# Weight sums of one stream in two steps, eight warming products, and a new written order

## The chip, the cores and the metric

One Trainium2 chip, one core of it. The metric is the device time of one execution in microseconds; the median of the runs shown is compared. The core has TensorE for matrix products (PE, with PEld for loading its stationary operand), VectorE (DVE), ScalarE (ACT), GpSimd (POOL) and SyncE (SP), which issues most of the DMAs. Products are written to PSUM, everything else lives in SBUF.

## The reference

A causal convolution in time with 15 taps and a spacing of 2, from 144 to 288 channels, over 2 sequences of 16000 positions; then the gate tanh(f) * sigmoid(g) on the two halves of the 288 channels, and a product with a 144 x 144 matrix. Inputs and output are bfloat16.

```python
xp = jnp.pad(x, ((0, 0), (pad, 0), (0, 0)))          # pad = 28
h = sum(einsum('btc,cd->btd', xp[:, pad-2*i : pad-2*i+T], w[i]) for i in range(15))
z = tanh(h[..., :144]) * sigmoid(h[..., 144:])
out = z @ w_o
```

## The kernel before, in words

The positions are cut into 11 blocks, and these into 21 units. A unit takes 128 runs of 12 positions each (one run per partition) through the convolution, the gate and the projection. The convolution is not computed tap by tap: it is split like a fast polynomial product. Sums and differences of shifted inputs are formed on VectorE, sums and differences of weights once at the start, and TensorE needs fewer products for the same result. The four streams are S, D, F and G. S works on the sum of two shifted inputs with the sums of the weights of taps j and j + 8 (G1); D on the differences (Gm); F and G on the difference E with the plain weights. Each stream has derived inputs (S2, S4, S42 and so on, made by `derive`) and derived weights:

- G1 (Gm for D): w[j] plus (minus) w[j + 8], for j = 0 to 6; the eighth is w[7] alone.
- H: G1[j] - G1[j + 4], for j = 0 to 3.
- HH: G1[j] - G1[j + 4] - G1[j + 2] + G1[j + 6], for j = 0 and 1.
- GD: G1[4h + j] - G1[4h + j + 2], for h and j = 0 and 1.

The weights of D, F and G are made by VectorE (`wsum`, line 550, "ws" in the order). Those of S are made by TensorE: `psum_sum` (line 560) multiplies plain weights with the identity or its negative, so that the sum comes up in a PSUM pair, and a cast on ScalarE puts it into SBUF ("wsum" in the order, first the products, then the cast). In the kernel before, each of the nine sums takes plain weights alone, and each waits for all four loads of w (`load_w`, line 529; slice q holds taps 4q to 4q + 3, the last slice three taps).

In a unit the steps of a stream k are named VVk (two products with HH), V2ak and V2bk (with H), cVVk and cVk (ScalarE's negated copies inside PSUM), AVk (with GD), A00k to A11k (with G1 or w; a last "r" marks the product with the rest channels), and evk, yk (results out of PSUM). The 16 input channels above 128 are kept apart: their sums ("st") are transposed and laid out as R. For block 0 that happens on TensorE (`sums_front`, line 403): 16 transposes ("trR", line 420), a copy of one half by ScalarE and one by VectorE ("cpR", line 427), and two products with zeros ("zR", line 432) that reset the PSUM pair, for r = 0 and again for r = 1. For other blocks it goes through DMAs (T, q, R). Wr holds the weights of the rest channels, loaded by 15 DMAs on POOL ("wrl"), wo_ab those of the projection ("wol"). "OP" is the projection, "os" its cast, "th", "sg" and "zm" the gate.

PSUM is divided into four pairs of banks; a step that opens a pair waits until all users of the pair's former content are done. The order on every engine's queue is a written list (`ORDER`, lines 33 to 116), one list each for PE, ACT, DVE, DMA (SP's queue), POOL and for the opening of pairs. A name is unit/step; unit -1 is the preparation. `place` (line 200) takes the steps by these lists. The costs and due times given to `add` made the lists, and they do not change which step follows which.

Ahead of everything TensorE runs warming products of zeros, 512 columns each (line 527).

Of the kernel before, what the change touches and what calls it, by code (L numbers as in the profile page):

```python
# [26 lines left out]
def t_dve(n, psum=False):  # L27
# [7 lines left out]
   -1/wsum#10 wsum#6 wsum#12 wsum#4 wsum#16 wsum#8 wsum#2 wsum wsum#14 0/VVF V2bF V2aF VVG -1/trR 0/V2aG V2bG A01F A11F -1/zR 0/A10F A00F A00G A11Fr  # L35
   A01G A10Fr A00Fr A10G A01Fr A11G A00Gr A01Gr 1/AVS 0/VVS A11Gr A10Gr AVS V2aS V2bS -1/trR#1 0/A00S A01S A11S A00Sr A01Sr -1/zR#1 0/A10S VVD A10Sr
   A11Sr AVD V2aD V2bD 1/VVS 0/A01D A00D A01Dr A00Dr 1/V2aS V2bS 0/A11D A10D A11Dr A10Dr 1/A00S A01S A10S AVD VVD A11S V2aD V2bD VVF A10D A11D A00D
   A01D V2bF V2aF VVG 2/AVS 1/A00F A01F V2bG V2aG A10F A11F A11G 2/VVS 1/A10G A00G 2/V2bS V2aS 1/A01G 2/AVD A01S A00S VVD A10S A11S V2bD V2aD 1/OP0
   2/VVF A11D A10D A00D A01D V2aF V2bF 3/AVD 2/VVG A01F A00F A10F V2bG V2aG A11F 1/OP1 2/A00G 3/VVS 2/A01G A11G A10G 3/V2aS V2bS AVS VVD A11S A10S V2bD
   V2aD A01S A00S VVF A01D A00D A11D A10D V2bF V2aF 2/OP0 3/VVG A11F A10F 4/AVS 3/V2bG V2aG A01F A00F 2/OP1 3/A00G 4/VVS 3/A01G A10G A11G 4/V2bS V2aS  # L40
   AVD VVD A10S A11S V2aD V2bD A00S A01S VVF A01D A00D A11D A10D V2bF V2aF 5/AVD 4/VVG A11F A01F A00F A10F V2bG V2aG 3/OP1 OP0 4/A00G 5/VVS 4/A01G
   5/AVS V2bS V2aS 4/A10G A11G 5/VVD A11S A10S V2bD V2aD A00S A01S VVF A00D A01D A10D A11D V2bF V2aF 4/OP0 5/VVG A01F A00F 6/AVS 5/A10F A11F V2aG V2bG
   4/OP1 6/VVS 5/A11G A10G A00G A01G 6/V2aS V2bS AVD VVD A10S A11S V2bD V2aD A01S A00S VVF A11D A10D A01D A00D V2aF V2bF 7/AVD 6/VVG A01F A11F A00F
   A10F V2aG V2bG 5/OP1 OP0 6/A11G 7/VVS 6/A10G 7/AVS V2aS V2bS 6/A00G 7/VVD 6/A01G 7/A00S V2aD V2bD A01S A10S A11S A11D VVF A10D A01D A00D V2bF V2aF
   6/OP0 7/VVG A10F A11F 8/AVS 7/A01F A00F V2bG V2aG 6/OP1 8/VVS 7/A00G A01G 8/AVD V2aS V2bS 7/A10G 8/VVD 7/A11G 8/A01S A00S V2bD V2aD A10S A11S VVF
   A01D A00D A11D A10D V2bF V2aF 9/AVD 8/VVG A01F A11F A10F A00F V2bG V2aG 7/OP1 OP0 8/A11G A10G 9/VVS 8/A01G A00G 9/V2aS V2bS AVS VVD A11S A10S V2aD
   V2bD A00S A01S VVF A00D A01D A10D A11D V2bF V2aF 8/OP0 9/VVG A01F A11F A00F A10F 10/AVS 9/V2bG V2aG 8/OP1 10/VVS 9/A01G A00G 10/AVD V2aS V2bS 9/A10G
   10/VVD 9/A11G 10/A01S V2aD V2bD A00S A10S A11S A11D VVF A10D A01D A00D V2aF V2bF 11/AVD 10/VVG A10F A00F V2aG A11F 9/OP1 10/A01F V2bG 9/OP0 11/VVS
   10/A10G A11G A01G A00G 11/V2aS V2bS AVS VVD A11S A10S V2bD V2aD A00S A01S VVF A10D A11D V2bF V2aF A01D A00D 10/OP0 11/A10F VVG A01F 12/AVS 11/A11F
   A00F V2aG V2bG 10/OP1 12/VVS 11/A00G A01G 12/AVD V2bS V2aS 11/A11G 12/VVD 11/A10G 12/A01S V2bD V2aD A00S A10S A11S A00D VVF A01D A11D A10D V2aF V2bF  # L50
   13/AVD 12/VVG A10F A01F A11F A00F V2bG V2aG 11/OP1 OP0 12/A11G 13/VVS 12/A10G 13/AVS V2bS V2aS 12/A00G 13/VVD 12/A01G 13/A11S V2aD V2bD A10S A00S
   A01S A00D A01D VVF A11D A10D 12/OP0 13/V2bF V2aF VVG 14/AVS 13/A01F V2aG A00F V2bG A10F A11F 12/OP1 13/A00G 14/VVS 13/A01G 14/AVD V2bS V2aS 13/A11G
   14/VVD 13/A10G 14/A01S A00S V2bD V2aD A10S A11S VVF A10D A11D A01D A00D V2bF V2aF 15/AVD 14/VVG A01F V2bG A10F V2aG A11F A00F A10G 13/OP1 OP0
   14/A11G 15/VVS 14/A00G A01G 15/V2bS V2aS AVS VVD A00S A01S V2bD V2aD A11S A10S VVF A10D A11D A00D A01D V2bF V2aF 14/OP0 15/VVG A01F A00F 16/AVS
   15/V2aG A10F V2bG 14/OP1 15/A11F A10G 16/VVS 15/A11G 16/AVD V2bS V2aS 15/A01G A00G 16/VVD A11S A10S V2bD V2aD A01S A00S VVF A10D A11D A01D A00D V2aF
   V2bF 17/AVD 16/VVG A00F V2aG V2bG A01F A11F A10F A00G A01G 15/OP1 OP0 17/VVS 16/A10G A11G 17/V2aS V2bS AVS VVD A11S A10S V2aD V2bD A01S A00S VVF
   A01D A00D A11D A10D V2aF V2bF 16/OP0 17/VVG A00F A01F A10F 18/AVS 17/V2aG V2bG A11F 16/OP1 17/A00G 18/VVS 17/A01G 18/AVD V2bS V2aS 17/A11G A10G
   18/VVD A10S A11S V2aD V2bD A01S VVF A00S A01D A00D A11D A10D V2aF V2bF 19/AVD 18/VVG A01F A00F A11F A10F V2aG V2bG 17/OP1 OP0 18/A00G 19/VVS 18/A01G
# [186 lines left out]
def kernel(  # L245
# [7 lines left out]
    nc = tc.nc  # L253
    P = 128
# [267 lines left out]
    warm = const.tile([P, 1], F32)  # L522
    K_(nc.gpsimd.memset(warm[:], 0.0))
    K_(nc.scalar.activation(out=warm[:], in_=warm[:], func=ACT.Sigmoid))
    NWARM = 15
    for i in range(NWARM):
        K_(nc.tensor.matmul(banks[i % 4][:, (i // 4) % 2, :], lhsT=wz[:, 0:P], rhs=wz[:], start=True, stop=True))  # L527

# [468 lines left out]
```

## Time and profile before

| what | us |
|---|---|
| median of 3 runs (312.89 to 314.5) | 313.0 |
| profiled execution | 313.12 |
| its span | 311.3 |
| TensorE busy | 297.5 |
| VectorE busy | 276.5 |
| ScalarE busy | 269.0 |

The span runs from the first to the last instruction; the execution's time holds 1.8 us around it. Line numbers (L491, L316) are those of the kernel before. L491 is the helper that issues nearly all products, L316 the one for nearly all of VectorE's sums, so rows are told apart by their tiles: "acc<-w_all,ident" is a weight sum, "acc<-wz" at L527 a warming product, "acc<-ident,T" at L420 a transpose for R. In the timeline a row gives the start, the length and what the engine waited for.

### The profile page before, as it was taken

The numbers are of one execution on the slowest core, as the hardware profiler recorded it, in microseconds if no ns is written. First come the engines' busy times: TensorE is split into PE (matmuls) and PEld (weight loads), VectorE is DVE, ScalarE is ACT, GpSimd is POOL, SyncE is SP. The second block draws the span as 40 slices with busy tenths as digits, with TensorE's granted clock in tenths as the row PEclk, the third lists the DMA queues.
The fourth block names the chain that finished last, engine by engine and source line by source line (L and its number), as shares of the span: only waits on it lengthen the run. The fifth ranks groups of instructions, "written<-read, shape, count | busy, mean of one in ns | idle before, by whom it ended". The sixth has DMA issues, their size and how long they took to land.

```text
span 311.3 us, 6703 instructions
## 1 busy us (share of the span) xinstructions
PE 297.5 (96%) x2604; PEld 276.5 (89%) x2604; DVE 276.5 (89%) x393; ACT 269.0 (86%) x449; POOL 27.0 (9%) x63
## 2 busy tenths in 40 slices
PE   8998899999999999999999999999999999999981
PEld 3797789999999999999999999999999999999881
DVE  4878999999999999899999999989996998899861
ACT  1658789998989989999998999989888999989982
POOL 9830500000000000000000000000000000000013
PEclk9999999999999999999999999999999999999997
DMA  7995569597799866986796698455886647254344
GB/s 199 107 127 118 150 67 174 140 115 153 126 162 282 215 159 104 142 199 155 189 210 98 118 181 182 138 127 162 146 187 80 123 141 231 73 128 114 59 170 131
DMA packets 153110, 45.78 MB, mean 147 GB/s; under 512 B 137061, under 2 KB 151701, under 8 KB 153078
## 3 DMA queue, kind: packets, MB, share of 16 engines
q1 hardware_dynamic: 151610, 44.59, 69.6%
q0 software_dynamic: 1216, 0.70, 1.1%
q8 instruction: 20, 0.33, 0.5%
q14 instruction: 12, 0.10, 0.1%
q10 hardware_dynamic: 252, 0.06, 0.1%
HBM read 13.31 MB, written 11.84 MB: 81 GB/s over the span
## 4 chain that ended last, share of the span: by engine, by line
PE 80%; ACT 13%; DVE 3%; issue 3%; DVEq 0%; ACTq 0%
PE acc L491 77%; ACT m L761 4%; ACT acc L683 3%; PE acc L527 2%; ACT acc L677 1%; ACT sg L746 1%; ACT th L744 1%; ACT R L427 1%; DVE D L316 1%; DVE S L316 1%; PE acc L420 1%; DVE y L316 1%; ACT os L882 0%; ACT av L695 0%; ACT osl L852 0%
## 5 line engine op out<-in xcount | busy, mean ns | idle before, releaser
L491 PEld LDWEIGHTS <-E 128*128 128x128 bf16 x882 | 112.2, 145 | 7.9 <-issue 4.0
L491 PE MATMUL acc<-w_all,E 128*128 128x288 bf16 x630 | 101.2, 286 | 1.0 <-ACT acc L683 0.3
L491 PE MATMUL acc<-Wr,R 128*128 128x288 bf16 x336 | 94.9, 286 | 0.0
L316 DVE TENSOR_TENSOR y<-U,acc 128x576 bf16<-128x576 bf16 (+1 forms) x81 | 59.4, 744 | 9.9 <-PE acc L491 6.5
L683 ACT ACTIVATE acc<-acc 128x576 f32<-128x576 f32 x84 | 54.1, 645 | 7.2 <-PE acc L491 4.9
L761 ACT ACTIVATE m<-acc 128x576 bf16<-128x576 f32 x84 | 52.8, 651 | 4.3 <-PE acc L491 2.9
L491 PEld LDWEIGHTS <-S 128*128 128x128 bf16 x378 | 48.2, 137 | 5.2 <-issue 2.4
L491 PEld LDWEIGHTS <-D 128*128 128x128 bf16 x378 | 48.8, 137 | 4.0 <-issue 1.1
L677 ACT ACTIVATE acc<-acc 128x288 f32<-128x288 f32 x84 | 33.7, 401 | 8.0 <-PE acc L491 6.4
L746 ACT ACTIVATE sg<-y 128x576 bf16<-128x576 bf16 (+3 forms) x45 | 38.9, 872 | 0.5 <-DVE y L316 0.4
L744 ACT ACTIVATE th<-y 128x576 bf16<-128x576 bf16 (+3 forms) x45 | 38.9, 871 | 0.2
L882 ACT CAST os<-acc 128x864 bf16<-128x864 f32 x40 | 34.6, 880 | 2.0 <-DVE y L316 0.9
L316 DVE TENSOR_TENSOR m<-m,av 128x1152 bf16<-128x1152 bf16 x42 | 30.5, 753 | 6.5 <-ACT m L761 6.3
L491 PE MATMUL acc<-wo_ab,zT 128*128 128x144 bf16 x480 | 35.2, 226 | 0.1
L491 PEld LDWEIGHTS <-zT 128*128 128x128 bf16 x480 | 32.2, 98 | 1.5 <-issue 0.3
L491 PEld LDWEIGHTS <-R 128*128 128x128 bf16 x336 | 32.8, 98 | 0.2
L491 PE MATMUL acc<-G,S 128*128 128x288 bf16 x147 | 30.3, 286 | 0.4 <-ACT acc L683 0.2
L491 PE MATMUL acc<-Gm,D 128*128 128x288 bf16 x147 | 29.7, 285 | 0.3
L695 ACT ACTIVATE av<-acc 128x576 bf16<-128x576 f32 x42 | 27.2, 648 | 3.0 <-PE acc L491 2.4
L491 PE MATMUL acc<-H,E 128*128 128x288 bf16 x168 | 28.1, 286 | 1.1 <-ACT acc L677 1.1
L316 DVE TENSOR_TENSOR E<-E 128x1792 bf16<-128x1792 bf16 (+1 forms) x22 | 28.1, 1286 | 0.0
L316 DVE TENSOR_TENSOR z<-th,sg 128x576 bf16<-128x576 bf16 (+3 forms) x45 | 25.5, 573 | 2.1 <-ACT sg L746 1.4
(75 smaller groups left out, 330.0 us busy)
## 6 DMA issues: line engine op xcount, KB each, us to landing
R<-q SPq DMA_DIRECT2D x19, 512.0 KB
out_dram<-os SPq DMA_DIRECT2D x8, 864.0 KB
q<-T SPq DMA_DIRECT2D x10, 256.0 KB
out_dram<-os SPq DMA_DIRECT2D x2, 519.8 KB
xt<-in_x_dram SPq DMA_DIRECT2D x6, 156.0 KB
w_all<-in_w_dram SPq DMA_DIRECT2D x3, 288.0 KB
out_dram<-os SPq DMA_DIRECT2D x2, 337.5 KB
zT<-z SPq DMA_TRANSPOSE x20
```

The lines of the kernel that those rows point to most:

```text
L316: return K_(nc.vector.tensor_tensor(out=out_, in0=a, in1=b, op=op))
L420: K_(nc.tensor.transpose(to, ap(st.tile, c, [1, P]), ident[:, 0, :]))
L427: K_(nc.vector.tensor_copy(out=dst, in_=src) if h else nc.scalar.copy(out=dst, in_=src))
L491: K_(nc.tensor.matmul(bank, lhsT=l(), rhs=r, start=start and q == 0, stop=end and q == len(jobs) - 1, skip_group_check=True))
L527: K_(nc.tensor.matmul(banks[i % 4][:, (i // 4) % 2, :], lhsT=wz[:, 0:P], rhs=wz[:], start=True, stop=True))
L677: add("ACT", t_act(D2), lambda: K_(nc.scalar.activation(out=banks[X.slot][:, 1, 0:D2], in_=banks[X.slot][:, 0, 0:D2], func=ACT.Copy, scale ...
L683: s = add("ACT", t_act(2 * D2), lambda: K_(nc.scalar.activation(out=banks[Y.slot][:, :, 0:D2], in_=banks[X.slot][:, :, 0:D2], func=ACT.Cop ...
L695: add("ACT", t_act(2 * D2), lambda: K_(nc.scalar.activation(out=av.tile[:, SPLIT.index(k)], in_=banks[W.slot][:, :, 0:D2], func=ACT.Copy, ...
L744: add("ACT", t_act(n * D, False), lambda: K_(nc.scalar.activation(out=a_, in_=y_[0], func=ACT.Tanh)), r=[*need, y], w=[th], want=t0, name= ...
L746: add("ACT", t_act(n * D, False), lambda: K_(nc.scalar.activation(out=b_, in_=y_[1], func=ACT.Sigmoid)), r=[*need, y], w=[sg], want=t0 + . ...
L761: add("ACT", t_act(2 * D2), lambda pair=pair, i=i, b2=b2: K_(nc.scalar.activation(out=m.tile[:, i, 2 * b2:2 * b2 + 2, :], in_=banks[pair.s ...
L882: K_(nc.scalar.copy(out=dst, in_=banks[pr.slot][:, :, 0:3 * D].rearrange("p h (q d) -> p h q d", d=D)))
```

## The change

Four things are changed together.

- Eight warming products instead of 15.
- The weight sums of S in two steps. The first makes G1 from plain weights: taps 0 to 3 need slices 0 and 2, taps 4 to 6 need slices 1 and 3, and each waits for those two alone. The second makes HH, H and GD from G1, read back from SBUF, with one product per term.
- `load_w` has other planning costs and due times and is called for slices 0, 2, 1, 3.
- All lists of `ORDER` are written anew: the front differs most, the units by the places of single steps. In the DMA list the names count the calls, so that "w w#3 w#1 w#2" is now slices 0, 3, 2, 1, where "w w#2 w#1 w#3" was 0, 2, 1, 3.

The first lines of the lists, before and after:

```diff
 PE:
-   -1/wsum#10 wsum#6 wsum#12 wsum#4 wsum#16 wsum#8 wsum#2 wsum wsum#14 0/VVF V2bF V2aF VVG -1/trR 0/V2aG V2bG A01F A11F -1/zR 0/A10F A00F A00G A11Fr
+   -1/wsum wsum#4 wsum#2 wsum#6 wsum#8 wsum#10 wsum#12 wsum#14 wsum#16 0/VVF V2aF V2bF VVG A11F V2aG -1/trR 0/A00F A01F V2bG -1/zR 0/A10F A11Fr A00Fr
 ACT:
-   -1/wsum#7 wsum#13 wsum#5 wsum#11 wsum#17 wsum#9 wsum#3 hc wsum#1 0/cVVF -1/wsum#15 0/cVF cVVG -1/cpR 0/cVG y1F y0F y0G cVVS y1G eAVS cVS -1/cpR#2
+   -1/hc wsum#1 wsum#5 wsum#3 wsum#7 wsum#11 wsum#9 wsum#13 wsum#17 wsum#15 0/cVVF cVF cVVG -1/cpR 0/cVG y1F y0F y0G y1G cVVS eAVS cVS -1/cpR#2 0/ev1S
 DVE:
-   -1/ws ws#8 ws#1 ws#6 ws#9 ws#10 E ws#2 ws#5 ws#3 E#1 E2 ws#4 ws#11 stS stD stE E4 cpR#1 S ws#7 1/stD -1/D S4 1/stS -1/D4 wr S2 S42 1/stE -1/D42 wr#1
-   cpR#3 D2 0/E 1/S 3/stE stS 1/S2 S4 0/av0 3/stD 0/av1 1/D 0/U y1 y#1 1/D4 0/y 1/av0 av1 U y0F 0/zm4 zm0 1/y1F y1 y1G S42 y0G D2 D42 2/E 0/E2 E4 2/av0
+   -1/ws ws#9 ws#1 ws#6 ws#2 ws#5 ws#11 E ws#8 ws#10 E#1 E2 E4 stD stS stE D cpR#1 ws#7 S ws#3 S4 D4 S2 S42 0/E -1/wr ws#4 cpR#3 wr#1 D2 1/stD stS stE
+   -1/D42 1/S S4 S2 3/stS stD 0/av0 av1 1/D 0/U y1 1/S42 3/stE 0/y y#1 1/av0 av1 U 0/zm4 1/y0F 0/zm0 1/y1 y1F D4 y1G y0G D2 zm4 D42 0/E2 E4 2/E av0 av1
 DMA:
-   -1/w w#2 w#1 w#3 xn xt xn#1 xt#1 xt#2 xt#3 xt#4 xt#5 0/xt -1/xn#2 1/T 0/xn 1/q R 2/xt 0/zT 4/xt#4 2/xn 3/T 1/R#1 3/q 1/zT 4/xn 5/T 6/xt#5 xt#2 3/R
+   -1/w w#3 w#1 w#2 xn xn#1 xt#1 xt#3 xt#2 xt xt#5 xn#2 xt#4 0/xt 1/T 0/xn 1/q R 3/T 0/zT 1/R#1 2/xt xn 3/q 6/xt 1/zT 4/xt#1 3/R#1 R 4/xt 5/T 4/xt#4
 POOL:
-   -1/wrl#10 wrl#9 wrl#5 wrl#1 wrl wz wol#14 wrl#4 wol#10 wo72 wol#2 wrl#13 wol#13 wrl#7 wrl#6 wol#9 wrl#11 wol#5 wrl#12 wrl#3 wrl#2 wrl#14 wol#8 wrl#8
+   -1/wrl#3 wrl#11 wrl#5 wrl#1 wrl#10 wrl#7 wrl#9 wrl#13 wz wol#5 wol#6 wrl#8 wol#1 wrl#14 wol wol#12 wrl#6 wrl#4 wrl#2 wrl wrl#12 wo72 wol#8 wol#2
```

The end of the lists of PE and DVE:

```diff
 PE:
-   19/OP1 20/A01F A11F A10F V2bG V2aG A00F 19/OP0 20/A00G A01G OP0 OP1 tr#1 A10G A11G OPe#2 tr OPe#1 tr#2 OPe tr#3 tr#4 OPe#4 OPe#3 OPe#5
+   A01F A00F V2bG 19/OP0 20/A01G A00G OP0 OP1 tr#1 A10G OPe#2 tr A11G OPe#1 tr#2 OPe tr#3 tr#4 OPe#4 OPe#3 OPe#5
```

The code:

```diff
-    NWARM = 15
+    NWARM = 8
...
-            w=[gw[q]], want=-28.5 + q / 10, name="w")
-
-    for q in range(4):
+            w=[gw[q]], want=-29.5 + q % 2 / 5 + q / 20, name="w")
+
+    for q in (0, 2, 1, 3):
         load_w(q)
...
-                mms(banks[pr.slot][:, q, 0:D2], [((lambda n_=n_: ident[:, n_, :]), w_all[:, j, :]) for n_, j in t_])
+                mms(banks[pr.slot][:, q, 0:D2], [((lambda n_=n_: ident[:, n_, :]), v) for n_, v in t_])
...
-        return [(0, j)] + ([(i, j + 8)] if j + 8 < K else [])
-
-    def minus(i, j):
-        return [(1, j)] + ([(1 - i, j + 8)] if j + 8 < K else [])
+        return [(0, w_all[:, j, :])] + ([(i, w_all[:, j + 8, :])] if j + 8 < K else [])
...
-        wall = [*gw.values()]
+        wa, wb = [gw[0], gw[2]], [gw[1], gw[3]]
...
-        psum_sum(HH[:, i], [plus(i, j) + minus(i, j + 4) + minus(i, j + 2) + plus(i, j + 6) for j in range(2)], wall, [gHH[k]], wt)
-        psum_sum(H[:, i, 0:2], [plus(i, j) + minus(i, j + 4) for j in (0, 1)], wall, [gH[k]], wt + .2)
-        psum_sum(H[:, i, 2:4], [plus(i, j) + minus(i, j + 4) for j in (2, 3)], wall, [gH[k]], wt + .1)
+
+        psum_sum(g[:, 0:2], [plus(i, j) for j in (0, 1)], wa, [gG[k, 0]], wt)
+        psum_sum(g[:, 4:6], [plus(i, j) for j in (4, 5)], wb, [gG[k, 1]], wt + .1)
+        psum_sum(g[:, 2:4], [plus(i, j) for j in (2, 3)], wa, [gG[k, 0]], wt + .2)
+        psum_sum(g[:, 6:7], [plus(i, 6)], wb, [gG[k, 1]], wt + .3)
+        of = lambda j: g[:, j, :] if j < 7 else w_all[:, 7, :]
+        both = [gG[k, 0], gG[k, 1], gw[1]]
+        psum_sum(HH[:, i], [[(0, of(j)), (1, of(j + 4)), (1, of(j + 2)), (0, of(j + 6))] for j in (0, 1)], both, [gHH[k]], wt + .4)
+        psum_sum(H[:, i, 0:2], [[(0, of(j)), (1, of(j + 4))] for j in (0, 1)], both, [gH[k]], wt + .5)
+        psum_sum(H[:, i, 2:4], [[(0, of(j)), (1, of(j + 4))] for j in (2, 3)], both, [gH[k]], wt + .6)
         if k in SPLIT:
             for h in range(2):
-                psum_sum(GD[:, SPLIT.index(k), h], [plus(i, 4 * h + j) + minus(i, 4 * h + j + 2) for j in range(2)], wall, [gGD[k]], wt + .25)
-        psum_sum(g[:, 4:6], [plus(i, j) for j in (4, 5)], wall, [gG[k, 1]], wt + .3)
-        psum_sum(g[:, 6:7], [plus(i, 6)], wall, [gG[k, 1]], wt + .35)
-        psum_sum(g[:, 0:2], [plus(i, j) for j in (0, 1)], wall, [gG[k, 0]], wt + .4)
-        psum_sum(g[:, 2:4], [plus(i, j) for j in (2, 3)], wall, [gG[k, 0]], wt + .5)
+                psum_sum(GD[:, SPLIT.index(k), h], [[(0, of(4 * h + j)), (1, of(4 * h + j + 2))] for j in range(2)], both, [gGD[k]], wt + .7 + h / 10)
```

The sums that the nine names of TensorE's list stand for, wsum#2n for the n-th call: before, HH, H (0, 1), H (2, 3), GD twice, G1 (4, 5), G1 (6), G1 (0, 1), G1 (2, 3); after, G1 (0, 1), G1 (4, 5), G1 (2, 3), G1 (6), HH, H (0, 1), H (2, 3), GD twice.

More of the change, by code (lines that the diff above doesn't have):

```diff
@@ L34 @@
 PE:
[L35 to L58, printed above, removed]
@@ L95 @@
[L95 to L101 removed]
+   -1/wsum wsum#4 wsum#2 wsum#6 wsum#8 wsum#10 wsum#12 wsum#14 wsum#16 0/VVF V2aF V2bF VVG A11F V2aG -1/trR 0/A00F A01F V2bG -1/zR 0/A10F A11Fr A00Fr
@@ new lines @@
+   A01Fr A10Fr A00G A01G A11G A01Gr A00Gr A10G A11Gr A10Gr 1/AVS 0/VVS AVS V2bS V2aS -1/trR#1 0/A10S A11S A00S A10Sr A11Sr A01S -1/zR#1 0/A00Sr VVD AVD
+   A01Sr V2aD V2bD 1/VVS 0/A00D A01D A00Dr A01Dr 1/V2bS V2aS 0/A10D A11D A10Dr A11Dr 1/A10S A11S A00S AVD VVD A01S V2aD V2bD VVF A00D A01D A11D A10D
+   V2bF V2aF VVG A10F A01F A00F V2aG V2bG A11F 2/AVS 1/A10G A11G 2/VVS 1/A00G A01G 2/V2aS V2bS AVD VVD A01S A00S A10S A11S V2bD V2aD 1/OP0 2/VVF A11D
+   A10D A00D A01D V2bF V2aF 3/AVD 2/VVG A00F A10F A01F V2aG V2bG A11F 1/OP1 2/A00G A01G 3/VVS 2/A11G A10G 3/V2aS V2bS AVS VVD A10S A11S V2bD V2aD A00S
```

122 lines of the change are left out of this document (70 added, 52 removed).

## The prediction

> **What bounds the kernel now.** I read the head of the page first, then the busy time by stage, then who waits for whom.
>
> ```profile
> span 311.3 us, 6703 instructions
> ```
>
> ```profile
> 14.46:30.00 15.54, 13.84 (x124) 12.48 (x123) 13.15 (x21) 10.84 (x19) 3.77 (x8) 1.00 0.83 107
> 30.00:50.00 20.00, 18.16 (x140) 16.23 (x140) 18.87 (x28) 17.15 (x32) 4.73 (x9) 1.00 0.70 126
> 50.00:290.00 240.00, 238.83 (x2131) 228.03 (x2129) 224.85 (x309) 221.60 (x364) 1.57 (x6) 1.00 0.72 152
> 290.00:306.50 16.50, 13.45 (x144) 11.79 (x141) 10.45 (x21) 13.46 (x29) 3.74 (x6) 1.00 0.52 156
> ```
>
> Columns: stretch, its length, then busy time of PE, PEld, DVE, ACT, POOL, granted clock, DMA share, GB/s. From 50 to 290 us TensorE stands still for 1.17 of 240 us. So what makes the front end earlier on TensorE comes out one for one at the end, and what does not is worth nothing. The front has 1.70 us of idle TensorE between 14.46 and 30 and 1.84 between 30 and 50; before 14.46 it is busy, but with warming products and weight sums.
>
> What TensorE waits for up to 45 us (the two longest after the start), then from 45 to 290:
>
> ```profile
> PE acc L432 <- DVE R L427: 1.0, 2, 0.8
> PE acc L491 <- ACT acc L677: 0.7, 2, 0.5
> ```
>
> ```profile
> PE acc L491 <- ACT os L882: 0.2, 1, 0.2
> ```
>
> So the front is held by chains through ScalarE and VectorE too. Its rows from the timeline (start, length), TensorE and then VectorE's first sums:
>
> ```profile
> 1.19 6.20 PE L527 MATMUL acc<-wz 128*128 128x512 bf16 x15 [1.19 <-DVE wz L521]
> 7.23 7.39 PE L491 MATMUL acc<-w_all,ident 128*128 128x288 bf16 x59
> 14.46 0.41 PE L491 MATMUL acc<-HH,E 128*128 128x288 bf16 x2
> 15.42 0.65 PE L491 MATMUL acc<-H,E 128*128 128x288 bf16 x4 [0.55 <-ACT acc L677]
> ...
> 16.15 1.06 PE L420 MATMUL acc<-ident,T 128*128 128x128 bf16 x16
> ...
> 19.03 0.41 PE L432 MATMUL acc<-wz 128*128 128x288 bf16 x2 [0.25 <-DVE R L427]
> ```
>
> ```profile
> 4.64 0.76 DVE L554 TENSOR_TENSOR Gm<-w_all 128x1152 bf16<-128x1152 bf16 x1 [2.04 <-DMA w_all<-in_w_dram]
> 5.87 0.76 DVE L554 TENSOR_TENSOR H<-w_all 128x1152 bf16<-128x1152 bf16 x1 [0.47 <-DMA w_all<-in_w_dram]
> 6.56 0.61 DVE L554 TENSOR_TENSOR Gm<-w_all 128x864 bf16<-128x864 bf16 x1
> ```
>
> Fifteen warming products end at about 7.2, the 59 products of S's weight sums fill 7.23 to 14.46 (0.1225 us each), and only then unit 0 begins. The warming products run at half of that rate: 6.20 us for 15, the last of which is already short, is 0.427 us for 512 columns, so 0.24 for 288. The clock column says 1.00 all the same; by the products the step to the full rate lies at about 7.0.
>
> **The change, part by part.**
>
> *Warming, 15 to 8.* At 0.427 us they end at 1.19 + 3.42 = 4.61 instead of 7.2. That is worth only what can start then.
>
> *Weight loads.* On SP the written order goes from slices 0, 2, 1, 3 to 0, 3, 2, 1. By VectorE's rows slices 0 and 2 are there at 4.64, 1 at 5.87, 3 by 6.56; a slice of four taps takes 1.23 us, so the three-tap one 0.92. With slice 3 ahead, slice 2 comes at 4.64 + 0.92 = 5.56, the last at 6.5 as now. So the first step waits for the third load: it starts at 5.65, after a gap of 1.0 us on TensorE. VectorE's first sum slips by 0.9 too; a wait of 0.47 stands behind it, and one of 0.93 before E (below), and these take it up.
>
> *Weight sums, 59 products to 38.* From the code: now 15 (HH), 8 + 7 (H), 8 + 7 (GD), 14 (G1); then 14 (G1), 8 (HH), 8 (H), 8 (GD). 21 fewer are 2.57 us. The price is that step two reads G1 from SBUF, behind four casts. Half rate to 7.0 gives 5.6 products, the other 8.4 take 1.0: step one ends at 8.0.
>
> ScalarE's casts, then VectorE's sums of x (tile E) and of the channel rest xt:
>
> ```profile
> 10.54 1.19 ACT L572 CAST G<-acc 128x576 bf16<-128x576 f32 x2
> ```
>
> ```profile
> L316 DVE TENSOR_TENSOR E<-xn x3: 949/958/1749, 9.3 to 28.2; 128x1536 bf16<-128x1536 bf16 x2, 128x3072 bf16<-128x3072 bf16 x1
> L316 DVE TENSOR_TENSOR E<-E x2: 1094/1288/1481, 12.3 to 15.2; 128x1792 bf16<-128x1792 bf16 x1, 128x2560 bf16<-128x2560 bf16 x1
> its engine sat idle before it (us, times) until:
>   DMA xn<-in_x_dram: 0.9, 1
> ```
>
> ```profile
> 14.49 0.76 DVE L316 TENSOR_TENSOR T<-xt 128x256 bf16<-128x256 bf16 x3 [0.37 <-issue]
> ```
>
> Two casts take 1.19, one starts 0.55 after the other. G1's four end at 8.9; step two starts at 9.0 (TensorE idle for 1.0 again) and its 24 products, 2.94 us, end at 11.94. The casts of its five sums start at 10.55, after the first of H as written, and end at 13.3.
>
> *Unit 0.* VVF needs both halves of E. The first waits for its load at 9.33 as now; behind it stand two weight sums (0.69 + 0.38), the second half (0.95), E2 (1.0), E4 (1.4) and the xt sums (0.7), each its length less some 0.07 by which the next starts early: E at 12.25, E2 at 13.25, E4 at 14.65, xt at 15.35. So VVF starts at 12.35, not 14.46. But its copy on ScalarE stands behind the casts, at 13.3, so V2aF comes at 13.75, not 15.42. Then cVF (to 14.95), A11F (15.0 to 15.5), V2aG, and the transposes trR at 15.75, not 16.15: E4 and A11F now stand ahead of them, and the lead shrinks from 2.1 to 0.40.
>
> *The R chains.* The chain of waits for block 0's second R:
>
> ```profile
> 25.11 0.91 PE acc L420 x16
> 26.02 0.02 issue
> 26.05 1.02 ACT R L427
> 27.07 0.02 issue
> 27.09 0.70 DVE R L427
> 27.79 0.04 issue
> 27.83 0.41 PE acc L432 x2
> ```
>
> VectorE's half of the copy starts only when ScalarE's is done, though another half of the bank. The same chain takes 19.03 - 16.15 = 2.88 for the first R, and in the new order no VectorE work pushes it (D ends at 16.5, ahead of the copy at 17.9): zR at 18.63, with A00F's four products (0.49) already behind TensorE. Behind zR it took 5.92 us to the second transposes (24.95; the chain counts from 25.11, when the products ahead have drained). Less 0.49 for A00F and 0.25 of waiting for S2 that goes, this is 5.2, so 23.85. VectorE supplies that if S and its sums come in time:
>
> ```profile
> L316 DVE TENSOR_TENSOR S<-S x5: 619/816/953, 21.6 to 33.0; 128x1536 bf16<-128x1536 bf16 x2, 128x768 bf16<-128x768 bf16 x2, 128x1280 bf16<-128x1280 bf16 x1
> ...
> L316 DVE TENSOR_TENSOR S<-xn x2: 1215/1220/1226, 18.9 to 30.8; 128x2048 bf16<-128x2048 bf16 x2
> ```
>
> Copy to 18.6, two small sums, S (1.15), S4 (0.87), D4, S2, S42: S4 at 21.0, S2 at 22.6, needed at 21.9 and 23.1. Then block 1's E (1.75, to 25.0), moved ahead of the second copy, and two weight sums: 25.5, when ScalarE's half ends at 26.0, so E hides. Second zR: 23.85 + 2.88 = 26.73 instead of 27.83, with two more products (0.25) done before it. Lead: 1.10 + 0.25 = 1.35 us.
>
> *Moved transfers.* Block 1's transpose of x on SP goes ahead of two xt transfers, one of which waits for VectorE's sums of block 0.
>
> ```profile
> 16.39 6.04 SPq L343 DMA_TRANSPOSE xn<-in_x_dram  x1
> ```
>
> It is done at about 22.4 now and only earlier then, so block 1's E does not wait. xt of block 0 keeps its place after xn to within one small transfer; if it lands 0.5 late, trR is 0.1 late, for E4 covers it. On POOL eight instead of five loads of Wr precede the clearing of wo_ab, which nothing reads before unit 0's projection. POOL's issues, and a Wr load's landing:
>
> ```profile
> 15.09 1.93 POOL L540 DMA_DIRECT2D Wr<-in_w_dram  x4 [0.34 <-DMA wo_ab<-in_w_o_dram]
> ```
>
> ```profile
> Wr<-in_w_dram POOLq DMA_DIRECT2D x15, 9.0 KB, 3.8
> ```
>
> The last load of Wr's first half is the third of these four, at 16.05, so it lands near 19.9; it moves from the 20th to the 19th place, 19.4, and A11Fr now wants it at 19.4: between 0 and 0.5 late; I take 0.
>
> *Units 1 to 19 and the end.* Only orders change, with the same work. The one answer for 30 to 50: at best its 1.84 of idle goes, at worst as much comes; I take 0, since the same three engines are at 18.2, 18.9 and 17.2 of 20. For 50 to 290: a gain of 1.17 at most, a loss of 4.0 if each of 20 units gets one wait of 0.2, the only one shown there; 0, as nearest to today's row. At the end the last A11G goes behind the transposes of another group:
>
> ```profile
> 299.76 0.41 PE L844 MATMUL acc<-ident,z 128*72 128x128 bf16 x4
> ```
>
> That is between -0.4 and +0.4; 0.
>
> *Sum.* The profiled execution took 313.12 (span 311.3, 1.8 around it), the median is 313.0. 313.12 - 1.35 = 311.8.
>
> The Trainium skill ("TensorE: Matmul & The Clock Gate", Part 1) says that the half-rate clock is released after a free-running window of about 3.4 us of sustained activity, whenever that window falls. Our trace agrees that it is time and not a count, as the release at 7.0 came after 5.8 us; whether a gap of 1.0 us spoils a window no run here shows. By that rule a spoiled window would put the release at an estimated 10.4, and the sum at about 312.6.
>
> **The rivals.**
> *The gap keeps the clock down.* Now TensorE is never idle from 1.19 to the release at 7.0. If the gap starts that count of 5.8 us anew at 5.65, the full rate comes at 11.45: step one ends at 9.0, step two starts at 9.65 and ends at 13.5, its casts at 14.8, V2aF at 15.25, 1.5 later than forecast. That eats the lead: 313.2. For it: nothing but warming filled the half-rate stretch. Against: two thirds of the time is busy anyway.
> *All of the removed work comes out.* First real product 1.58 earlier, 2.57 fewer, less 0.7 for six at half rate: 3.4, so 309.7. It needs the R chains and the idle between 14.46 and 30 to shrink beyond my walk; the fixed 2.88 speaks against it.
> *The new orders cost a wait in every unit.* Place: 50 to 290, where VectorE and ScalarE are at 94% and 92% and any swap can put a copy behind its reader. Price at 0.2 per unit: 4.0, so 315.8. From 0.07 a unit the gain is gone; from 0.15 on the kernel is over 0.5% slower. Against: the sequences per unit differ mostly by swaps of neighbours.
> *It is hidden anyway.* If xt or the copies keep zR at 19.0 and 27.8: 313.1.
>
> **How the numbers follow.** 0.5% (1.57 us) is about what a measurement of this kernel can tell from no change. Forecast 0.46, its own range 311.1 to 312.4, about a third of it under 311.43; clock 0.15; hidden 0.06; full gain 0.18; unit orders 0.15. Faster: 0.18 + 0.16 = 0.34; slower 0.15; same 0.51. The range takes in the full gain and the two cases of no change, with 0.5 for the open ends: 309.4 to 313.9.
>
> **What would show it.** 38 products of the weight sums, starting near 5.65, with a gap of about 1 us before them and one near 8 to 9; half-rate ones among the first; VVF near 12.4 and V2aF near 13.8; zR near 18.6 and 26.7; TensorE idle near 1.2 between 50 and 290. I am wrong if the products are half-rate past 8, if zR has not moved, or if waits appear in the units.

## The result: slower by 0.47%, and the profile after

The changed kernel takes 314.5 us (median of 20 runs, 312.42 to 315.85), the kernel before 312.98 (20 runs beside it, 312.48 to 314.5). The ratio is 1.0047, 95% interval 1.0034 to 1.0059. The forecast of 311.8 us had the wrong sign, and 314.5 lies above its range.

The runs of the changed kernel fall into two groups by their mean granted clock: 8 have 0.992 or more and a median of 313.8, 12 have 0.987 to 0.990 and 314.9, 1.1 us more. Of the 85 runs of the kernel before that stand beside the experiments, 15 have 0.989 or 0.990 and none less, and they take 0.2 us more than the other 70 (313.2 and 312.9). A mean lower by 0.005 over 312 us is 1.6 us of clock, which is 3.2 us at half rate. The half-rate tail after the last product lowers the mean too, so this split is a hint; the experiments below show the stretch itself, in kernels with the same weight sums. The profiled run took 313.51 us and belongs to the first group, so its rows show what is lost without the second effect.

A part of the loss is in no row. The execution's time holds 2.07 to 2.17 us around the span in every run of the changed kernel, and 1.73 to 1.86 in each of those 85 runs of the kernel before. So 0.34 of the 1.5 us lie outside the span, and inside it the medians are 312.4 and 311.2. All kernels below that have the new front (the part of the lists up to the end of unit 1's F and G products) have the 2.1, whatever their warming, load order, POOL list or units, and all that have the old front the 1.8, with two-step weight sums too. Which of the front's lists brings it, and at which end of the span it lies, no run shows.

The page of the profiled run, and its busy time by stage (columns as in the prediction):

```profile
span 311.4 us, 6652 instructions
```

```profile
14.46:30.00 15.54, 13.35 (x120) 12.13 (x120) 12.82 (x23) 9.85 (x16) 4.87 (x10) 1.00 0.73 83
30.00:50.00 20.00, 17.99 (x136) 16.07 (x136) 19.18 (x29) 16.90 (x31) 3.19 (x6) 1.00 0.80 164
50.00:290.00 240.00, 238.20 (x2127) 227.45 (x2126) 225.30 (x308) 221.54 (x363) 1.61 (x6) 1.00 0.72 151
```

TensorE stands idle for 2.19 us between 14.46 and 30 (before 1.70), 2.01 up to 50 (1.84) and 1.80 up to 290 (1.17). The timeline of TensorE in the front:

```profile
1.19 3.59 PE L526 MATMUL acc<-wz 128*128 128x512 bf16 x8 [1.19 <-DVE wz L520]
4.58 0.44 PE L490 MATMUL acc<-w_all,ident 128*128 128x288 bf16 x1
5.88 3.28 PE L490 MATMUL acc<-w_all,ident 128*128 128x288 bf16 x13 [0.85 <-DMA w_all<-in_w_dram]
8.95 1.59 PE L490 MATMUL acc<-G,ident 128*128 128x288 bf16 x7
...
12.51 0.47 PE L490 MATMUL acc<-HH,E 128*128 128x288 bf16 x2
14.35 0.65 PE L490 MATMUL acc<-H,E 128*128 128x288 bf16 x4 [1.37 <-ACT acc L676]
14.84 0.41 PE L490 MATMUL acc<-HH,E 128*128 128x288 bf16 x2
15.79 0.65 PE L490 MATMUL acc<-w_all,E 128*128 128x288 bf16 x4 [0.54 <-ACT acc L682]
16.27 0.41 PE L490 MATMUL acc<-H,E 128*128 128x288 bf16 x2
16.52 1.06 PE L419 MATMUL acc<-ident,T 128*128 128x128 bf16 x16
...
19.40 0.41 PE L431 MATMUL acc<-wz 128*128 128x288 bf16 x2 [0.59 <-DVE R L426]
...
27.64 0.40 PE L431 MATMUL acc<-wz 128*128 128x288 bf16 x2 [0.55 <-DVE R L426]
```

The gap before the third load is there (0.85, 0.1 from the forecast). Then come 13 products, and the row behind them starts 3.07 later: 0.24 each, half rate throughout, and the last products of step two start at 12.34 instead of 11.8. V2aF is at 14.35, not 13.75, the transposes at 16.52, not 15.75 (before 16.15), the first zR at 19.40, not 18.63 (before 19.03), the second at 27.64, not 26.73 (before 27.83). Unit 1's VVS, the first step behind all of this, starts at 30.18 against 30.31: a lead of 0.13, not 1.35.

Between 45 and 290 there is one new wait:

```profile
PE acc L490 <- ACT acc L682: 0.6, 1, 0.6
```

In the timeline it stands in unit 20, and the kernel before has one as long on ScalarE just behind 290, which the changed kernel has not; the rows of the kernel after and of the one before:

```profile
289.82 0.41 PE L490 MATMUL acc<-Gm,D 128*128 128x288 bf16 x2 [0.62 <-ACT acc L682]
```

```profile
291.44 0.65 PE L491 MATMUL acc<-H,E 128*128 128x288 bf16 x4 [0.58 <-ACT acc L677]
```

So the 0.63 more of idle time up to 290 is nearly all an exchange. The lead of 0.13 is given back between 30 and 50 (0.17 more of idle time). The rest of the loss, above all that of the 12 other runs, had to be found by experiment.

### The profile page after: what moved, and what is told of

It is laid out like the page before. It is cut to its first block, busy times and chain, and to the rows that moved or that the text cites. A ratio compares the mean times of both kernels' runs of the same rounds, so it can differ in the third digit from the quotient of the medians.

```text
span 311.4 us, 6652 instructions
## 1 busy us (share of the span) xinstructions
PE 294.9 (95%) x2576; PEld 274.2 (88%) x2576; DVE 276.5 (89%) x393; ACT 269.4 (87%) x449; POOL 27.0 (9%) x63
## 4 chain that ended last, share of the span: by engine, by line
PE 76%; ACT 15%; DVE 3%; issue 2%; DMA 1%; POOL 1%; SPq 0%; POOLq 0%; ACTq 0%
PE acc L490 75%; ACT m L760 5%; ACT acc L682 3%; ACT acc L676 2%; ACT sg L745 1%; DVE y L315 1%; DMA w_all<-in_w_dram 1%; ACT th L743 1%; ACT os L881 1%; POOL out_dram L913 1%; ACT R L426 1%; PE acc L419 1%; DVE R L426 0%; ACT av L694 0%; ACT H L571 0%
```

## The experiments

Four theories are weighed. **A**: the gap ahead of the weight sums delays the release of the clock. **B**: the new orders of the units, or of the end, cost it. **C**: the front alone costs it, since TensorE now has its weight sums done early, stands idle until E is there, and the clock falls back. **D**: more loads of Wr at the head of POOL's list slow the loads of w and x. Medians are set beside 313.0 to 313.1 of the kernel before, run beside them on the same chip.

### The gap (A)

Closed by 15 warming products, or by 11, or shortened by the old order of the loads; and the reverse, the gap put into the kernel before.

```diff
-    NWARM = 8
+    NWARM = 15
```

> The changed kernel with 15 warming products again, everything else as changed. Theory A (the gap on TensorE ahead of the weight sums delays the release of the full clock, by a different amount from run to run): no gap any more, so the step to the full rate comes near 7 us, before the first weight sum, in nearly every run; median 313.0 to 313.6 and runs within about 1 us of each other, mean granted clock near 0.993 in all. Theory B (the new orders of the units and the end cost the time): the front's clock does not matter, median 314.3 to 314.8, spread as in the changed kernel (2 us and more).

```diff
-    NWARM = 8
+    NWARM = 11
```

> The changed kernel with 11 warming products, which at 0.427 us each end at 5.89, when the third load of weights is there. Theory A: TensorE is busy without a gap up to about 9 us, the full rate comes near 7 us, step one ends near 8 instead of 9.2, and the median is 312.4 to 313.2, the best of these kernels. Theory B: 314.3 to 314.8, as the changed kernel.

```diff
 DMA:
-   -1/w w#3 w#1 w#2 xn xn#1
+   -1/w w#1 w#2 w#3 xn xn#1
```

> The changed kernel with the four weight loads issued for slices 0, 2, 1, 3 as before the change, nothing else. Slices 0 and 2 are there at 4.64, so the gap after the eighth warming product is under 0.2 us and step one starts at about 4.7 instead of 5.88. Theory A: full rate near 7 us in most runs, median 312.4 to 313.3. Theory B: 314.2 to 314.8.

The kernel before, with

```diff
-    NWARM = 15
+    NWARM = 8
```

> The kernel before with 8 warming products instead of 15, nothing else. The weight sums wait for all four loads, so there is a gap on TensorE from 4.6 to about 6.6 us. Theory A: the release of the full clock slips to 10 us or later, many of the 59 products run at 0.24 us, median 314 to 316 and a spread of 2 us and more. Theory B: the gap is harmless and the sums start 0.6 us earlier, median 312.4 to 313.0.

Measured: with 15 warming products 313.76 us (1.0037, 1.0021 to 1.0053), with 11 314.91 (1.0059, 1.0040 to 1.0079), with the old load order 314.33 (1.0047, 1.0026 to 1.0067); the kernel before with eight 314.18 (1.0041, 1.0026 to 1.0055). The last is what A foresees. In its timeline the weight sums run at half rate well past 7 and end 0.8 us late:

```profile
5.93 0.40 PE L491 MATMUL acc<-w_all,ident 128*128 128x288 bf16 x1 [1.14 <-DMA w_all<-in_w_dram]
6.64 8.81 PE L491 MATMUL acc<-w_all,ident 128*128 128x288 bf16 x58 [0.31 <-DMA w_all<-in_w_dram]
15.29 0.41 PE L491 MATMUL acc<-HH,E 128*128 128x288 bf16 x2
```

But in the changed kernel taking the gap away does not clearly help. All three medians lie above what theory A foresaw, and the intervals of all three ratios overlap that of the changed kernel (1.0047). Low mean clocks are still there: with 15 warming products in 5 of 12 runs (median 315.1, the others 313.5), with the old load order in 8 of 12 (315.3 and 313.1). With 11 the median is the worst of the three. Its TensorE in the timeline:

```profile
6.04 1.82 PE L490 MATMUL acc<-w_all,ident 128*128 128x288 bf16 x13 [0.20 <-DMA w_all<-in_w_dram]
...
11.13 0.29 PE L490 MATMUL acc<-w_all,ident 128*128 128x288 bf16 x1
13.23 0.47 PE L490 MATMUL acc<-HH,E 128*128 128x288 bf16 x2 [1.81 <-DVE E L315]
14.36 0.71 PE L490 MATMUL acc<-H,E 128*128 128x288 bf16 x4 [0.66 <-DVE E L315]
14.91 0.41 PE L490 MATMUL acc<-HH,E 128*128 128x288 bf16 x2
15.85 1.12 PE L490 MATMUL acc<-w_all,E 128*128 128x288 bf16 x4 [0.54 <-ACT acc L682]
16.77 0.69 PE L490 MATMUL acc<-H,E 128*128 128x288 bf16 x2
17.25 1.85 PE L419 MATMUL acc<-ident,T 128*128 128x128 bf16 x16
```

The weight sums are at full rate and done by 11.4. Then TensorE waits 1.81 for E, 0.66 for E2 and 0.54 for ScalarE, and from there the same four products take 1.12 instead of 0.65 and the transposes 1.85 instead of 1.06. The busy time in stretches of 3.41 us shows the clock (third column from the end) at half:

```profile
8.65:12.07 3.42, 2.77 (x23) 1.95 (x20) 2.69 (x6) 2.08 (x4) 3.13 (x7) 1.00 0.96 124
12.07:15.48 3.41, 1.43 (x8) 0.92 (x8) 3.38 (x4) 1.43 (x4) 3.24 (x7) 1.00 1.06 74
15.48:18.89 3.41, 3.04 (x22) 2.70 (x23) 2.07 (x5) 0.63 (x2) 3.33 (x7) 0.50 0.98 103
```

Five of its 6 runs have the low mean clock. So A holds where it was put into the kernel before, and is not what slows the changed one as a whole.

### The idle time ahead of E (C)

The kernel with 11 warming products, and 14 products of zeros in the place where TensorE stood idle:

```diff
         def vv():
+            for _ in range(14 if base == 0 and k == "F" else 0):
+                K_(nc.tensor.matmul(banks[X.slot][:, 0, 0:D2], lhsT=wz[:, 0:P], rhs=wz[:, 0:D2], start=True, stop=True))
             run(X, 0, [job(st, v - i, HH[:, i4, i, :]) for i in range(2)], True)
```

> The changed kernel with 11 warming products, as in the run with that number, and 14 more products of zeros ahead of unit 0's first product, where TensorE stood idle for 1.8 us waiting for E. Theory C: with the gap filled, fewer runs fall back to the half clock between 14 and 21 us; the mean granted clock is near 0.993 in most runs instead of 0.988 in five of six, and the median drops from 314.9 to 313.3 to 314.0, though work was added. Rival (the fall comes from the later gaps of 0.66 and 0.54 us, or is not due to idle time): no change, 314.6 to 315.2, or longer by up to 1.7 us.

Measured: 313.88 us (1.0022, 1.0011 to 1.0033), 1.03 less than without the zeros (there 1.0059, from 1.0040 up), and none of 7 runs has the low clock. The stretch in which the wait for E fell is now busy, and the next one, which holds the waits for E2 and ScalarE, is at 2.19 of 3.42 without a fall:

```profile
10.02:13.43 3.41, 3.41 (x29) 2.57 (x27) 2.86 (x4) 2.81 (x5) 3.41 (x7) 1.00 1.08 85
13.43:16.85 3.42, 2.19 (x15) 1.66 (x15) 3.39 (x7) 1.33 (x3) 2.81 (x7) 1.00 0.99 59
```

Added work made the kernel faster, as only C has it. Since E comes no earlier, the front gains nothing else by it.

### The units (B), and the loads on POOL (D)

The kernel before with the changed lists from the end of unit 1's F and G on (first line of PE's list shown; the other lists are cut at the same place):

```diff
-   A01D V2bF V2aF VVG 2/AVS 1/A00F A01F V2bG V2aG A10F A11F A11G 2/VVS 1/A10G A00G
+   A01D V2bF V2aF VVG A10F A01F A00F V2aG V2bG A11F 2/AVS 1/A10G A11G 2/VVS 1/A00G A01G
```

> The kernel before with its own front (weight sums, 15 warming products, all lists up to the end of unit 1's F and G products), and the changed kernel's lists from there to the end. Theory C (the front alone carries the change: idle TensorE ahead of E lets the clock fall back, and x lands later): the units cost nothing or little, median 312.8 to 313.3, the same as before. Theory B (the new orders of the units and the end): 313.8 to 314.6, and all of the loss is here.

The changed kernel with the old lists from there on:

```diff
-   V2bF V2aF VVG A10F A01F A00F V2aG V2bG A11F 2/AVS 1/A10G A11G 2/VVS 1/A00G A01G
+   V2bF V2aF VVG 2/AVS 1/A00F A01F V2bG V2aG A10F A11F A11G 2/VVS 1/A10G A00G
```

> The changed kernel's front just as changed (8 warming products, its load order), with the lists of the kernel before from the end of unit 1 on. Undoes the units alone. If the two losses add up: 314.5 less 0.7, 313.6 to 314.1, undisturbed runs near 313.1 and runs with a fall of the clock near 314.3. If the units cost only what they cost beside the old front: 314.3 or more.

The changed kernel with the old list of POOL:

```diff
 POOL:
-   -1/wrl#3 wrl#11 wrl#5 wrl#1 wrl#10 wrl#7 wrl#9 wrl#13 wz wol#5
+   -1/wrl#10 wrl#9 wrl#5 wrl#1 wrl wz wol#14 wrl#4 wol#10 wo72
```

> The changed kernel with the list of POOL from the kernel before, so that five instead of eight loads of Wr run beside the loads of w and x; nothing else. Theory D (these loads slow w and x, so that E comes late): the first sum of E starts at 9.3 to 9.8 instead of 9.5 to 10.6, the third load of w lands at 5.6 instead of 5.9 to 6.4, and the median drops by 0.3 to 0.8, to 313.7 to 314.2. Rival (the landing is random and the Wr loads are too small to matter): 314.3 to 314.8.

Measured: the new units behind the old front 313.68 (1.0022, 1.0013 to 1.0030), all of its 11 runs at the high clock. That is below theory B's range and above theory C's: behind the old front the new orders cost 0.69 us, and not in every unit. The waits of TensorE between 30 and 50:

```profile
PE acc L490 <- ACT acc L676: 0.9, 2, 0.7
PE acc L490 <- ACT acc L682: 0.9, 2, 0.7
```

The kernel before has 0.2 and 0.5 there for the same two lines. The counter-test did not give the 0.7 back: 315.4 us (1.0066, 1.0043 to 1.0089), with the low clock in 5 of 6 runs. Its profiled run fell for two stretches on end, and unit 1's VVS started at 32.61, more than the units could return. What the new orders cost behind their own front, the traces show. From the start of unit 1's VVS to the end of the span the kernel before takes 311.3 - 30.31 = 281.0 us, the changed kernel 311.4 - 30.18 = 281.2, and so do five other traces with both the new front and the new orders (with the old POOL list 281.5); the new orders behind the old front take 311.5 - 29.76 = 281.7. The old orders do not fit the new front either: in the counter-test unit 3's VVS starts 60.59 - 32.61 = 27.98 behind unit 1's, in the kernel before 57.82 - 30.31 = 27.51. So each set of orders loses about 0.5 behind the other's front, and 0.2 is what the new one costs behind its own. The old POOL list changed nothing: 315.04 (1.0056, 1.0041 to 1.0071), and E's first sum starts at 10.17, where the changed kernel's profiled run has 9.46. D falls.

### The two steps by themselves

The kernel before with the two-step code alone, 15 warming products, and in its lists only the weight sums and their casts put in the new order:

```diff
 PE:
-   -1/wsum#10 wsum#6 wsum#12 wsum#4 wsum#16 wsum#8 wsum#2 wsum wsum#14 0/VVF V2bF V2aF VVG -1/trR
+   -1/wsum wsum#4 wsum#2 wsum#6 wsum#8 wsum#10 wsum#12 wsum#14 wsum#16 0/VVF V2bF V2aF VVG -1/trR
```

> The weight sums in two steps alone: the changed kernel's code with 15 warming products and the lists of the kernel before, in which only the weight sums and their casts stand in the new sequence; loads for slices 0, 2, 1, 3 as before. Theory C: the products start at 7.3, step two ends near 12.8, V2aF starts near 14.6 instead of 15.4, zR near 18.2 instead of 19.0; if the gaps stay small the gain reaches the end, 312.1 to 312.7; where the clock falls back in a run, that run takes 1.3 to 2 us more. Rival (E and the copies of R hold the front whatever the sums do): 312.8 to 313.3.

The same with zeros where TensorE would be idle: 4 ahead of HH, 6 ahead of VVF, 4 ahead of the transposes:

```diff
+            for _ in range(zeros):
+                K_(nc.tensor.matmul(banks[pr.slot][:, 0, 0:D2], lhsT=wz[:, 0:P], rhs=wz[:, 0:D2], start=True, stop=True))
```

> The weight sums in two steps with the lists of the kernel before (as in the run of the two steps alone, median 313.04, half of its runs with a fall of the clock), and products of zeros in three gaps: 4 ahead of HH, 6 ahead of unit 0's first product, 4 ahead of the first transposes. Theory C: the fall disappears, all runs near the 312.76 of the undisturbed half, median 312.5 to 312.9, a little faster than the kernel before. Rival (the two steps gain nothing by themselves): 312.9 to 313.3; or the fillers wait for a free PSUM pair and do not fill, then half of the runs stay at 313.9.

And the changed front with loads 0, 2, 1, 3, nine warming products, 4 zeros ahead of HH and 14 ahead of VVF, and the old lists behind it:

```diff
-    NWARM = 8
+    NFILL = 14
+    NWARM = 9
```

> The changed kernel's front, with loads for slices 0, 2, 1, 3, 9 warming products, 4 products of zeros ahead of HH and 14 ahead of unit 0's first product, and the lists of the kernel before from the end of unit 1's F and G products on. If the parts add up: 313.15 (undisturbed runs with that load order) less 0.69 (the units' new order) gives 312.3 to 312.8, with no fall of the clock, faster than before by 0.1 to 0.2%. If the changed front itself holds the loss: 313.2 or more.

Measured: the two steps alone 313.04 (1.0005, 0.9993 to 1.0018), 6 of 12 runs at the low clock with a median of 313.9, the other six 312.8. With zeros 312.85 (0.9992, 0.9981 to 1.0004), 10 of 12 at the high clock. This is the best kernel seen, and equal to the one before within its error. Its profiled run (312.34 us, the fastest of the 12) has what the prediction wanted:

```profile
12.49 0.47 PE L493 MATMUL acc<-HH,E 128*128 128x288 bf16 x2 [0.19 <-DVE E L316]
13.62 0.71 PE L493 MATMUL acc<-H,E 128*128 128x288 bf16 x4 [0.66 <-DVE E L316]
...
15.08 1.08 PE L422 MATMUL acc<-ident,T 128*128 128x128 bf16 x16
...
17.99 0.41 PE L434 MATMUL acc<-wz 128*128 128x288 bf16 x2 [0.18 <-DVE R L429]
...
29.54 0.41 PE L493 MATMUL acc<-HH,S 128*128 128x288 bf16 x2 [0.36 <-ACT av L705]
```

Transposes 1.07 earlier than before, zR 1.04, unit 1's VVS 0.77, and the span ends 0.8 earlier. That is a lucky run: over all 12 the median span is only 0.15 shorter (311.05 and 311.2). The third kernel missed its expectation: 313.62 (1.0024, 1.0009 to 1.0039), with 3 of 12 runs at the low clock. A part of the miss is the 0.3 outside the span that comes with the new front. Its profiled run had nearly the same start of unit 1 (29.60), but lost nearly 0.5 of its 0.7 up to 58 us (unit 3's VVS is at 57.57, before at 57.82). Between 30 and 50 a line that had 0.2 before now has

```profile
PE acc L490 <- ACT acc L684: 0.7, 2, 0.6
```

### A test of the rule

The trace also keeps when the granted clock changed. Relative to the first instruction, in us, with the least busy share of TensorE in any stretch of 3.413 us counted on from the release up to 21:

```
kernel                        release  least busy share  fall   back
before                           6.88     0.84             -      -
after                            9.93     0.55             -      -
15 warming                       7.12     0.65             -      -
11 warming                       5.24     0.42           15.48  18.89
before, 8 warming                9.83     0.84             -      -
old load order                   3.86     0.36           14.10  20.93
new units only                   5.06     0.84             -      -
11 warming and zeros             6.61     0.64             -      -
old POOL list                   10.02     0.59             -      -
two steps alone                  5.40     0.47           15.64  19.05
two steps with zeros             4.52     0.75             -      -
new front, zeros, old units      5.60     0.65             -      -
new front, old units             4.20     0.35           14.44  21.27
```

Each of these falls comes 10.24 us after the release, which is three times 3.413, and lasts 3.413 or 6.827. In each case the stretch that ends with the fall is the one with the least share, 0.35 to 0.47; the least share without a fall is 0.50 (the first stretch of the last row). The phase of this grid differs from run to run: the release of kernels with 15 warming products lies anywhere from 4.52 to 7.12. From this a last kernel was made with its outcome told beforehand: the changed kernel, its gap and eight warming products left alone, and 8 zeros ahead of VVF.

```diff
+    NFILL = 8
```

> The changed kernel with eight zero products (0.98 us at the full rate) ahead of unit 0's first two products, and nothing else: still eight warming products, still the old wait for the third load. The traces so far put every change of the clock on a grid of 3.413 us: a release at the end of the first stretch of the grid that TensorE was busy for 0.78 or more of, a fall at the end of one that it was busy for 0.47 or less of, none at 0.50 and 0.55. Where the grid lies differs from run to run. By this theory the gap ahead of the third load still splits the runs into early releases (about 3.8 to 5.8 us) and late ones (9.2 to 10.7), but the zeros take the idle of the worst stretch from about 2.1 to 1.2 us, so no run falls back: mean clock 0.9915 or more in all of them, against 8 of 20 before, and a median of 313.4 to 314.0. The profile shows no stretch at 0.50 between 14 and 21 us. If the fall has nothing to do with the idle time ahead of E, about 6 in 10 runs still show 0.987 to 0.990 and the median stays at 314.5.

Measured: 313.77 us (1.0022, 1.0013 to 1.0032), and none of 10 runs below 0.992. Its profiled run was an early release (4.18), of the kind that fell before, and the stretch that would have set the fall is the fourth row:

```profile
0.77:4.18 3.41, 2.98 (x8) 1.07 (x9) 1.15 (x2) 1.46 (x2) 3.33 (x15) 1.00 0.65 177
4.18:7.59 3.41, 2.08 (x16) 1.41 (x15) 1.53 (x3) 1.46 (x3) 3.41 (x8) 1.00 1.21 258
7.59:11.01 3.42, 3.02 (x25) 2.23 (x24) 2.91 (x7) 2.07 (x6) 3.13 (x4) 1.00 0.92 153
11.01:14.42 3.41, 2.13 (x16) 1.37 (x15) 3.34 (x5) 2.14 (x5) 3.41 (x8) 1.00 1.04 81
14.42:17.83 3.41, 2.87 (x33) 2.69 (x32) 2.84 (x5) 1.34 (x3) 3.41 (x8) 1.00 1.01 100
```

That is 2.13 of 3.41 busy, share 0.62, and no fall; without zeros, in the kernel with the old units and a release at 4.20, that stretch had

```profile
11.03:14.44 3.41, 1.21 (x9) 0.57 (x6) 3.34 (x5) 2.37 (x5) 3.41 (x7) 1.00 0.93 73
14.44:17.85 3.41, 2.81 (x11) 1.81 (x12) 3.41 (x6) 1.08 (x3) 3.33 (x7) 0.50 0.98 107
```

In the front it is the last stretch that tells these traces apart, and not the three from the release on together: here they have 0.61, 0.88 and 0.62, 2.11 in sum, without a fall, and in the two steps alone 0.91, 0.89 and 0.47, 2.27 in sum, with one.

The bound of 0.47 to 0.50 holds for the front only. All 14 traces fall once more on the same grid, at the end, where the products are short. There the clock fell after a stretch of 0.54 (new front, old units), 0.57 (two steps alone) and 0.63 (new front, zeros, old units), and did not after 0.63 (two steps with zeros) and 0.67 to 0.68 (old load order, new units only, before with 8 warming). So the busy share of the profile is near to what the clock follows, but not the same; between 0.50 and 0.63 it can go either way.

The Trainium skill ("TensorE: Matmul & The Clock Gate", Part 1) gives the window as 4096 cycles, 3413 ns, and free-running; the trace agrees, with changes 3.413, 6.827 and 10.24 apart. Its table ("Why this matters for your kernels") asks for no idle gaps over about 3 us; here it fell with no single gap above 1.91, so the measurement decides: what counts here is how busy a window was, and not one long gap.

## Why the prediction was wrong

- *"Half rate to 7.0"; the clock releases at 7.0.* Here it failed first. I took the release of one profiled run for a fixed time (and one release could not show that it is a time and not a count). It is the end of a window whose phase the program doesn't set: 3.86 to 10.02 in the runs shown. With the gap there are two cases. The first possible edge after the start of the warming lies within 3.413 us; as far as the rows show how much idle time a window bore before its release (0.74 yes, 0.85 no), edges from about 3.8 to 5.8 release early and the rest a whole window later, at 9.2 or more. That is an estimate of 0.58 to 0.42; the runs split 12 to 8 by their mean clock.
- *The late release* is the rival "the gap keeps the clock down", 0.15 and 313.2. It was right in kind for the profiled run: 9.93 against its 11.45, V2aF 14.35 against its 15.25. As the whole story it was not: such runs take 313.8.
- *"TensorE idle for 1.0 again" and VVF's wait for E.* Here it failed the second time, and this is the largest part, about half of the loss. I priced idle time of TensorE at its own length. With the early release it gathers ahead of E in one window, the clock falls back for 3.41 or 6.83 us, and what follows, from V2aF or the first A products to the transposes, runs at half rate: by the two groups of runs 314.9 - 313.8 = 1.1 us, by the zeros 1.03 and, from 314.5 to 313.77, 0.7 over all runs. The fall was traced in four kernels with two-step sums; the one trace of the changed kernel is of a late release. It does not carry the sign alone: with the zeros and no fall the changed kernel is still slower than the kernel before (1.0022, from 1.0013 up).
- *"Span 311.3, 1.8 around it".* The third failure: the sum kept the 1.8 as it was. It is 2.1 with the new front, 0.34 us more, and no run shows why.
- *Eight warming products, 4.61; the third load with a gap of 1.0.* Right: 4.58 and 0.85, though it moves (1.32 and 1.71 in other profiled runs).
- *The casts at 13.3, V2aF at 13.75, the lead of the transposes 0.40.* Off by 0.6 to 0.8, as step one ran at half rate to its end; A11F, put ahead of the transposes, then waits 0.54 for ScalarE's cVF, and the lead turned into a lag of 0.37.
- *The R chain, 2.88.* Right: 16.52 to 19.40 and 24.75 to 27.64 are 2.88 and 2.89; zR to the second transposes took 5.35 (5.2 forecast). Where the transposes do come early, as in the two steps with zeros, zR follows by 1.04.
- *Wr between 0 and 0.5 late, taken as 0.* Right: no wait of TensorE for Wr is among those of the front.
- *Units 1 to 19: 0.* Mis-sized: 0.2 behind the new front, and 0.69 behind the old one, most of it in 30 to 50. The bound of one wait per unit, 4.0, was far off.
- *21 products fewer are 2.57 us.* They are, but the end sees little of it: E's second half ends near 12.4 in the changed kernel and in the two steps with zeros (both start it at 11.5, for 0.95), so VVF cannot start before 12.5, and what was saved ahead of that is idle time. With the clock kept it is worth 0.2 us in the median (313.02 to 312.85, within the error).

What stays open: E's first sum starts at 9.33 to 9.86 with the old DMA list and at 9.46 to 10.58 with the new one, and POOL's list is not the cause. Of the 0.8 us that the changed kernel loses with the clock kept (313.8), 0.34 lie outside the span, without a known cause, and 0.2 in the units; the other 0.3 are not split between the late release and that landing.

## What to carry to other kernels

Before a change shortens TensorE's work ahead of a wait, add up TensorE's busy share over 3.4 us windows at every phase, since a window under about half busy halved the clock of the next here (at the end of a kernel one at 0.63 did too), even where no single gap is long. A saving that only makes TensorE wait for the same transfer can be worth less than nothing then; zero products in the wait were cheap insurance here. An order of steps that was planned behind one front is not a good one behind another. Compare the time outside the span too. And read a release or a fall of the clock in one profiled run as one draw of a phase, not as a time.

## What the runs showed of the hardware

- Adding 14 products (1.7 us of TensorE time) to the kernel with 11 warming products made it 1.03 us faster, and 8 added to the changed kernel 0.7.
- The clock column of a profile reads 1.00 before the first release, where the products run at 0.24 instead of 0.1225 us; after a later fall it reads 0.50.
- In the front of 14 profiled runs the clock fell once the busy share of a window was 0.47 or less, and never at 0.50 or more; at the end it also fell at 0.54, 0.57 and 0.63. In the front two falls lasted two windows (shares 0.79 and 0.82 in the first of these), two lasted one (0.89 and 0.98).
- The time outside the span is not fixed: 1.73 to 1.86 us with the old front, 2.07 to 2.18 with the new one, in all runs.
